# Attention, a spectral mix and an FFN on one core: one more chunk with seven block products, and a new order of the work

## Chip, cores and metric

The kernel runs on 1 core of one Trainium2 chip. The metric is the device time of one execution in microseconds, the median of several runs; a profile is one more execution, recorded by the hardware profiler.

## What is computed

Eight sequences of 576 positions, 8 heads of 64: windowed attention, whose output x (8 x 576 x 512) goes through a two-dimensional Fourier transform, a normalisation and an FFN of 512 to 2048 to 512. In float32 at the border:

```python
scores = np.where(mask, scale * np.matmul(q, k.transpose(0, 1, 3, 2)), -1e9)   # 0 <= row - col < 64
attn = np.exp(scores - max); attn = attn / (sum + 1e-09)
x = np.matmul(attn, v)                      # then heads side by side: 8 x 576 x 512
mixed = np.real(np.fft.fft(np.fft.fft(x, axis=1), axis=2))
u = x + mixed
un = (u - mu) / np.sqrt(var + 1e-06)
out = u + np.maximum(un @ w_ch1, 0.0) @ w_ch2
```

## The kernel before

The 4608 positions are 36 tiles of 128 (T0 to T35) and 18 chunks of two tiles (c0 to c17). `attn_tile(T)` loads k, q and v, turns k and q by the head dimension, makes scores, softmax and the product with v, and a first butterfly along the model dimension. `fft(b)` makes the two Fourier stages of one of the eight sequences and writes them to DRAM; `norm_tile(T)` gathers them back, adds, normalises and turns the result into the FFN's left operand. The first eleven tiles and chunk 0 work in float32; everything later in pairs of float16 (a high and a low part), and a product of two such pairs is three passes of matmuls (`PASSES`).

`ffn(c)` is the plain chunk: 16 first-layer steps `one` (12 matmuls of 256 columns each, L1419), ReLU into a high part on ScalarE (L1428) and a low part on VectorE (L1431), 16 second-layer steps `second` (6 matmuls of 512 columns, L1400), and one scaled addition for each of the two tiles (L1454).

`ffn7(c)` takes the chunks from `SEVEN` on. The hidden layer is cut in 8 pairs j of hidden blocks (`HALF`), the positions in two tiles, the outputs in two halves: 2 x 2 blocks, multiplied with seven block products instead of eight. The first layer is the same 192 matmuls (L1573). For each j ScalarE makes the ReLU (L1584), four sums of blocks follow on VectorE or GpSimd (`sums`, L1589), a cast to the high part on ScalarE or VectorE (`h_hi`), the low part on VectorE or GpSimd (`h_lo`, L1597), and then 7 products x 3 passes of 256 columns (L1548). The ending combines the blocks with one ScalarE step and seven VectorE additions. The sums of weight blocks, four of eight per j, are made once by `weight_sums(j)` (`sums` L1493, `more` L1500 to L1503, high parts by the copy helper L506, low parts L1511) and lie in `tw`, in buffers that attention used before (the staging of q, k, v, `flex`, `qbuf`, `kst`); the hidden tiles lie in the rings `kq`, `pr`, `pt`, `xe` and `yT`, which attention and the spectral stages use too.

```python
PROD = {1: (0, 0, 0), 6: (4, 0, 1), 7: (5, 1, 0), 5: (3, 3, 1), 2: (2, 2, 0), 3: (6, 2, 1), 4: (1, 3, 0)}
groups = (((0, 1, 2, 3), (1, 6, 7, 5, 4, 2, 3), 10),)      # product numbers of a middle j
for c in range(SEVEN, NCH):
    ffn7(c)
```

Nothing is ordered at run time. Every step is entered by `op(engine, duration, priority, function, reads, writes, ...)` and gets a running number; the table `ORDER` is the sequence in which all steps are issued, and `SECOND` names the steps that take the second of their two allowed engines. Every engine, and SyncE's queue with all its transfers, works its steps off in that order. `follow` walks the table and keeps the planner's own gap for each step; before the FFN begins, a planned gap of PE over 0.8 us is filled with matmuls into an unused bank (`warm`, L1759). Line numbers of the changed kernel are one higher behind the table.

Of the kernel before, what the change touches and what calls it, by code (L numbers as in the profile page):

```python
# [58 lines left out]
SEVEN = 12  # L59
# [339 lines left out]
def attn_fft_ffn_kernel(ctx: ExitStack, tc: tile.TileContext, q, k, v, w1, w2, gidx, dft_d, dft_s, mask, out):  # L399
# [1311 lines left out]
    for T in range(NTT):  # L1711
# [6 lines left out]
        if n in (4, 8):  # L1718
            base += FFT_AT + (FFT1 if T == 8 else 0)
            fft(2 * pb + n // 8, base)  # L1720
            for i, m in enumerate(range(0, 4) if n == 4 else range(4, 9)):
                args = NT * pb + m, base + NORM_AT + i + (EARLY if T == 4 and i > 1 else 0)
                if args[0] // 2 >= SEVEN + 4:
                    behind.setdefault(args[0] // 2, []).append(args)
# [66 lines left out]
```

## Time and profile before

| | us |
|---|---|
| median of 3 runs (944.35 to 948.38) | 944.51 |
| the profiled execution | 945.16 |
| its span, first to last instruction | 943.4 |
| TensorE matmul (PE) busy | 924.2 |
| VectorE (DVE) busy | 705.3 |
| GpSimd (POOL) busy | 441.5 |
| ScalarE (ACT) busy | 435.1 |

The busy times overlap each other. PE is TensorE's matmuls, PEld its loads of the stationary operand, SP the queue that issues nearly all transfers. A line such as `L1400 PE MATMUL po<-ws,hh` names the source line, the engine, and the tile written from the tiles read. The granted clock is given as a share of the full one; the DMA share is the mean busy share of the core's 16 DMA engines.

### The profile page before, as it was taken

To read this page: it belongs to the slowest core of one execution; us is meant where nothing else is said; L and a number is where in the kernel's file an instruction comes from. 1 tells how busy PE (TensorE), PEld (TensorE's weight loads), DVE (VectorE), ACT (ScalarE), POOL (GpSimd) and SP (SyncE) were. 2 spreads that over 40 slices of the span, in tenths; PEclk is the share of its full clock that TensorE was granted. 3 is DMA by queue.
4 is the path that set the end of the run, shared out by engine and by line. 5 is a ranking of instruction groups with operands and counts; after the bars stand their busy time and mean duration, and the time that the engine had idled before them with its cause. 6 is when DMAs were issued, how large, how long until landed. Compare 5 with 4: busy or idle time off the path is not lost.

```text
span 943.4 us, 24809 instructions
## 1 busy us (share of the span) xinstructions
PE 924.2 (98%) x9717; PEld 703.2 (75%) x9717; DVE 705.3 (75%) x1982; ACT 435.1 (46%) x979; POOL 441.5 (47%) x823
## 2 busy tenths in 40 slices
PE   7799999999999999999999999999999999999998
PEld 6677777666766676666766676667779998888887
DVE  5898998887767866677658757888898965675664
ACT  6875777834555424445443543444334442422111
POOL 2653464744744555465746544655601454124012
PEclk9999999999999999999999999999999999999999
DMA  9997447999689969879979788785402032210100
GB/s 231 239 263 202 133 144 147 167 173 169 136 193 163 198 122 167 185 152 207 197 168 190 150 162 169 163 147 108 137 12 57 24 96 65 68 35 13 57 24 23
DMA packets 300230, 128.69 MB, mean 136 GB/s; under 512 B 277768, under 2 KB 278152, under 8 KB 300112
## 3 DMA queue, kind: packets, MB, share of 16 engines
q1 hardware_dynamic: 297248, 118.06, 59.6%
q0 software_dynamic: 2720, 8.92, 3.3%
q8 instruction: 76, 1.25, 0.6%
q14 instruction: 42, 0.34, 0.1%
q10 hardware_dynamic: 144, 0.13, 0.0%
HBM read 60.76 MB, written 19.94 MB: 86 GB/s over the span
## 4 chain that ended last, share of the span: by engine, by line
PE 83%; DMA 5%; DVE 4%; POOL 3%; SPq 2%; issue 2%; ACT 1%; POOLq 0%; DVEq 0%; ACTq 0%
PE ph L1419 22%; PE po L1400 22%; PE ph L1573 13%; PE po L1548 11%; PE pz L1061 3%; PE pg L1023 3%; PE pa L739 3%; PE psc L662 2%; DMA kn<-in_k 1%; POOL flex L516 1%; DMA ve<-va 1%; DMA qn<-in_q 1%; DMA pt<-flex 1%; SPq L1277 1%; PE py L850 1%
## 5 line engine op out<-in xcount | busy, mean ns | idle before, releaser
L1400 PE MATMUL po<-ws,hh 128*128 128x512 f16 (+1 forms) x1116 | 284.5, 391 | 0.5 <-issue 0.2
L1419 PE MATMUL ph<-room,ws 128*128 128x256 f16 x2112 | 256.1, 273 | 1.8 <-DVE hh L1431 1.8
L1419 PEld LDWEIGHTS <-ws 128*128 128x128 f16 x2112 | 205.3, 98 | 54.1 <-issue 2.8
L1400 PEld LDWEIGHTS <-hh 128*128 128x128 f16 x1056 | 101.1, 98 | 90.0 <-DVE hh L1431 0.7
L1573 PE MATMUL ph<-room,ws 128*128 128x256 f16 x1152 | 136.2, 273 | 0.0
L1573 PEld LDWEIGHTS <-ws 128*128 128x128 f16 x1152 | 112.6, 98 | 13.6
L1428 ACT ACTIVATE hh<-ph 128x512 f16<-128x512 f32 x88 | 52.3, 594 | 120.8 <-PE ph L1419 99.8
L685 ACT ACTIVATE pr<-pr,nm 128x128 f32<-128x128 f32 x288 | 91.2, 393 | 31.5 <-DVE nm L677 31.4
L1431 DVE SCALAR_TENSOR_TENSOR hh<-ph,hh 128x512 f16<-128x512 f32 x88 | 60.4, 686 | 36.6 <-ACT hh L1428 36.5
L1135 POOL DMA_INDIRECT mt<-md,gix x34 | 42.0, 1235 | 96.7 <-DVE mv L1163 81.5
L677 DVE CUSTOM_DVE_ANT_0 pr<-psc,mskb 128x128 f32<-128x128 f32 x288 | 65.0, 287 | 25.9 <-PE psc L662 19.7
L1584 ACT ACTIVATE hx<-ph 128x512 f32<-128x512 f32 x47 | 27.8, 595 | 113.3 <-PE ph L1573 103.7
L1589 DVE TENSOR_TENSOR hx<-hx 128x128 f32<-128x128 f32 x164 | 45.1, 318 | 37.8 <-ACT hx L1584 36.2
L1548 PEld LDWEIGHTS <-hh 128*128 128x128 f16 x658 | 64.4, 98 | 7.6
L1597 POOL TENSOR_TENSOR hl<-hx,hh 128x256 f16<-128x256 f32 (+1 forms) x40 | 28.0, 730 | 77.3 <-DVE hh L510 53.7
L516 POOL TENSOR_TENSOR up<-un,up 128x128 f16<-128x128 f32 x84 | 40.9, 516 | 46.3 <-ACT up L506 38.8
L516 POOL TENSOR_TENSOR flex<-pr,flex 128x128 f16<-128x128 f32 x92 | 42.5, 494 | 36.2 <-ACT flex L506 18.2
L1548 PE MATMUL po<-ws,hh 128*128 128x256 f16 x282 | 51.2, 273 | 0.0
L1597 DVE TENSOR_TENSOR hl<-hx,hh 128x896 f16<-128x896 f32 x37 | 40.4, 1097 | 7.8 <-ACT hh L506 6.5
L752 POOL TENSOR_TENSOR rc<-rc,mone 128x4 f32<-128x4 f32 x29 | 32.5, 1129 | 26.6 <-DVE rc L747 16.8
L739 PE MATMUL pa<-ve,pt 128*64 128x65 f16 (+1 forms) x776 | 37.0, 203 | 2.5 <-ACT ve L506 1.8
L1548 PE MATMUL po<-ws,hl 128*128 128x256 f16 x141 | 38.4, 273 | 0.0
(244 smaller groups left out, 1718.6 us busy)
## 6 DMA issues: line engine op xcount, KB each, us to landing
room<-in_moe_w_ch SPq DMA_DIRECT2D x20, 512.0 KB
flex<-in_moe_w_ch SPq DMA_DIRECT2D x12, 512.0 KB
ve<-va SPq DMA_DIRECT2D x47, 130.0 KB
flex<-in_v SPq DMA_DIRECT2D x22, 256.0 KB
xs<-xu SPq DMA_DIRECT2D x22, 256.0 KB
xv<-xs SPq DMA_DIRECT2D x22, 256.0 KB
out<-xv SPq DMA_DIRECT2D x21, 256.0 KB
md<-mp SPq DMA_DIRECT2D x24, 192.0 KB
```

Of the source, the lines that this page charges most:

```text
L516: eng.tensor_tensor(out=out[:, k : k + w], in0=in0[:, k : k + w], in1=in1[:, k : k + w], op=al)
L677: nc.vector.tensor_tensor_reduce(out=t["pr", g][:, hp], in0=t["ps", g][:, hp], in1=mskb[:, m : m + P], scale=-0.125, scalar=3.0e38, op0=AL ...
L685: nc.scalar.activation(pr, pr, AF.Exp, bias=t["nm", g][:, hp : hp + 1], scale=-1.0)
L739: nc.tensor.matmul(pa[sl, hp], pt[:, sl], v_, start=(x == 0), stop=(x == len(mm) - 1))
L1400: nc.tensor.matmul(t["po"][i], l_, r_, start=(f == 0 and x == 0), stop=(f == NKF - 1 and x == len(mm) - 1))
L1419: nc.tensor.matmul(ph, l_, r_, start=(x == 0), stop=(x == len(mm) - 1))
L1428: nc.scalar.activation(t["hh", j][:, 0], ph, AF.Relu)
L1431: nc.vector.scalar_tensor_tensor(out=hh[:, 1], in0=ph, scalar=0.0, in1=hh[:, 0], op0=ALU.max, op1=ALU.subtract)
L1548: nc.tensor.matmul(t["po", bk][:, x], t["h", j][a][:, slot], right(n, j, b_), start=(j == 0 and k == 0 and n in opens), stop=(j == seven - ...
L1573: nc.tensor.matmul(ph, l_, r_, start=(x == 0), stop=(x == len(mm) - 1))
L1589: eng.tensor_tensor(out=x[:, o], in0=x[:, p0], in1=x[:, p1], op=al)
L1597: eng.tensor_tensor(out=lo[:, a:b_], in0=x[:, a + 1 : b_ + 1], in1=hi[:, a:b_], op=ALU.subtract)
```

## The change

`SEVEN` goes from 12 to 11, so chunk 11 is made by `ffn7` instead of `ffn`. With it the steps are numbered anew (3195 instead of 3178), the tables `ORDER` and `SECOND` are replaced as a whole, and no other line of the program differs. The first rows of the old and the new table:

```diff
@@ -56,151 +56,152 @@
 PASSES = ((0, 0), (0, 1), (1, 0))
 ONE = ((0, 0),)
-SEVEN = 12
+SEVEN = 11
 AWAY = 14
 
 ORDER = [int(i) for i in """
...
-1 115 0 9 7 116 3 15 118 119 120 145 121 124 144 129 16 149 125 130 173 126 131 147 150 117 127 148 17 132 21 18 176 153
...
+116 7 115 0 120 118 3 119 121 15 124 125 129 144 147 145 149 150 16 126 127 117 130 131 132 9 122 148 153 137 154 174
...
```

What the tables say, step by step: 69 steps of chunk 11 come and 52 go; 378 of the steps that both have change their engine, most between VectorE, ScalarE and GpSimd in attention, the spectral stages and the normalisation. Among PE's steps (771 before, 766 after) the first 140, up to the scores of T11, are the same work in nearly the same order. Behind them attention stands earlier: the scores of T24 have 348 PE steps ahead of them instead of 353, those of T30 444 instead of 460, those of T35 513 instead of 541. The first step of `weight_sums` stands beside chunk 9's FFN instead of chunk 10's.

## Rows read from the trace of the kernel before

**Rows 1.** The page: span and TensorE's busy time

```profile
span 943.4 us, 24809 instructions
...
PE 924.2 (98%) x9717; PEld 703.2 (75%) x9717; DVE 705.3 (75%) x1982; ACT 435.1 (46%) x979; POOL 441.5 (47%) x823
```

**Rows 2.** Busy time by stretch: opening, rest (stretch, length, engines with instruction counts, clock, DMA share, GB/s)

```profile
0.00:88.00 88.00, 77.05 (x949) 59.65 (x949) 69.61 (x267) 62.51 (x158) 45.19 (x83) 1.00 0.95 239
88.00:943.40 855.40, 847.14 (x8769) 643.52 (x8768) 635.68 (x1716) 372.64 (x822) 396.32 (x740) 1.00 0.60 126
```

**Rows 3.** PE's waits behind 88 us (us in total, times, longest)

```profile
PE ph L1419 <- DVE hh L1431: 1.8, 3, 1.3
PE psc L662 <- issue: 1.3, 3, 0.6
PE pa L739 <- DMA ve<-va: 0.5, 1, 0.5
...
```

**Rows 4.** The chain that ended last, its last piece (start, us, what)

```profile
939.45 0.75 DVE xv L1663
```

**Rows 5.** The same chain, one second-layer piece of each kind

```profile
621.96 2.59 PE po L1400 x12
...
712.22 2.29 PE po L1548 x21
```

**Rows 6.** Instruction groups by line (shapes, count, busy us, mean ns, idle before)

```profile
L1431 DVE SCALAR_TENSOR_TENSOR hh<-ph,hh 128x512 f16<-128x512 f32 x88 | 60.4, 686 | 36.6 <-ACT hh L1428 36.5
L1589 DVE TENSOR_TENSOR hx<-hx 128x128 f32<-128x128 f32 x164 | 45.1, 318 | 37.8 <-ACT hx L1584 36.2
L1597 DVE TENSOR_TENSOR hl<-hx,hh 128x896 f16<-128x896 f32 x37 | 40.4, 1097 | 7.8 <-ACT hh L506 6.5
L506 ACT CAST hh<-hx 128x896 f16<-128x896 f32 x24 | 22.5, 938 | 22.1 <-DVE hx L1589 21.3 <-POOL hx L1589 0.9
L1648 DVE SCALAR_TENSOR_TENSOR s<-po,osc,s 128x256 f32<-128x256 f32 x12 | 5.8, 481 | 1.2 <-ACT s L506 0.7
```

**Rows 7.** The tile of the weight sums (duration ns: min, median, max; first and last start)

```profile
L1493 DVE TENSOR_TENSOR td<-td,ws x16: 691/692/799, 614.2 to 723.5; 128x512 f32<-128x512 f32 x16
...
L1503 DVE TENSOR_TENSOR td<-td,ws x8: 424/424/536, 617.0 to 727.7; 128x256 f32<-128x256 f32 x8
L1511 DVE TENSOR_TENSOR flex<-td,flex x6: 677/684/691, 673.9 to 711.0; 128x512 f16<-128x512 f32 x6
```

**Rows 8.** Stretches around weight sums and chunk 12

```profile
620.00:740.00 120.00, 120.00 (x1126) 92.00 (x1125) 106.26 (x245) 45.69 (x92) 43.67 (x80) 1.00 0.36 82
...
720.00:740.00 20.00, 20.00 (x214) 18.13 (x213) 19.38 (x45) 8.26 (x13) 4.67 (x5) 1.00 0.14 33
```

**Rows 9.** The block sums by engine (duration ns: min, median, max)

```profile
L1589 DVE TENSOR_TENSOR hx<-hx x164: 280/287/760, 661.5 to 928.8; 128x128 f32<-128x128 f32 x164
L1589 POOL TENSOR_TENSOR hx<-hx x24: 449/456/1184, 765.6 to 923.3; 128x128 f32<-128x128 f32 x24
```

**Rows 10.** Stretches of attention: scores of T11 to T35, and two of 40 us

```profile
157.20:625.10 467.90, 463.73 (x5445) 326.70 (x5448) 342.12 (x1050) 224.45 (x538) 263.67 (x518) 1.00 0.87 169
160.00:200.00 40.00, 38.93 (x382) 25.40 (x380) 32.98 (x90) 28.59 (x57) 27.61 (x39) 1.00 0.96 163
...
440.00:480.00 40.00, 40.00 (x547) 29.90 (x545) 25.30 (x81) 20.16 (x53) 26.39 (x57) 1.00 0.99 191
```

**Rows 11.** The opening: a stretch, the weight conversions, the filler matmuls

```profile
40.00:50.00 10.00, 7.72 (x128) 5.80 (x126) 8.92 (x32) 7.68 (x19) 5.22 (x13) 1.00 1.06 282
...
L1289 DVE TENSOR_SCALAR ws<-room 128x1024 int32<-128x1024 int32 x10 | 7.1, 712 | 2.2 <-DMA room<-in_moe_w_ch 2.2
L1294 DVE SCALAR_TENSOR_TENSOR ws<-room,ws 128x1024 int32<-128x1024 int32 x10 | 12.4, 1238 | 0.3
L1301 DVE SCALAR_TENSOR_TENSOR ws<-room,ws 128x1024 uint16<-128x1024 uint32 x10 | 13.7, 1370 | 0.1
L1759 PE MATMUL warm<-ident 128*128 128x256 f16 x45 | 8.8, 325 | 1.5 <-POOL ident masks.py:199 1.5
```

277 rows, old and new, of tables (ORDER, SECOND) are left out of this document.

## The prediction

> **What bounds the kernel now.** I read the page's busy shares first, then stretches of the span, then what TensorE waited for, then the chain that ended last. The page says that TensorE (PE) is busy for 924.2 of 943.4 us [rows 1]. The stretches say where the other 19.2 us are: 10.95 before 88 us, in the opening, and 8.25 in the 855 us behind it, all at the full granted clock [rows 2]. What PE waited for behind the opening sums to about 4 us in waits of at most 1.3 us, most for the low half of the hidden layer (DVE hh) and for issue [rows 3]; the rest is the end, where the last VectorE step starts at 939.45 and the last transfer follows [rows 4]. So the kernel is its matmuls in sequence. An edit pays what it takes from PE, plus or minus what it does to 11 us of idle opening and 4 us of small waits; all other engines matter only where they begin to hold PE.
>
> The profiled execution took 945.16 us, of which 943.4 are the span; the median of the runs is 944.51, so 0.65 below it. I make the sum against 945.16 and take the 0.65 off at the end.
>
> **Part 1: chunk 11 takes seven products.** Its first layer keeps 192 matmuls of 256 columns. Its second layer had 16 steps of 6 matmuls of 512 columns; 12 such took 2.59 us, 0.216 each [rows 5], so 96 x 0.216 = 20.7. It becomes 8 x 7 products x 3 passes = 168 matmuls of 256 columns; 21 took 2.29, 0.109 each [rows 5]: 168 x 0.109 = 18.3. **PE: -2.4 us**, on the path, since PE has no wait there.
>
> The price is on the other engines. For each of 8 hidden blocks one VectorE low part of 0.69 goes; a sum step of 4 x 0.318 = 1.27 and a low part of 1.10 come, and ScalarE gets a cast of 0.94 [rows 6]: VectorE 8 x (2.37 - 0.69) = +13.4, ScalarE +7.5. The ending has seven output additions for two: three of 0.48, and four of 512 columns for two such, 0.69 each by the step that reads as much PSUM, some +3 [rows 6]. In the new table all eight of chunk 11's sum steps and low parts stand on VectorE. Cover: between the first step of the weight sums and the last low part that reads them, the old table has 145 VectorE steps beside 124.0 us of PE steps, the new one 135 steps beside 114.4. PE shrinks by 9.6 (eight FFN steps of 1.3 fewer, two attention products of 0.43 more); VectorE by only 5.1, at the mean durations of its rows. The weight sums themselves are the same (8 x (3 x 0.70 + 4 x 0.43 + 2 x 0.68)) [rows 7], only placed one chunk sooner. In the trace VectorE was busy 106.26 of 120 us from 620 to 740 while PE lost nothing, and 19.38 of 20 at the thickest [rows 8]. So 13.7 us of idle VectorE shrink by 9.6 - 5.1 = 4.5 to 9.2. I take this at nothing, because the row of 19.38 of 20 shows PE fed at a denser spot; if that cover is gone it costs up to 4.5.
>
> A trace row and a rule meet here. VectorE's sum instruction has a median of 287 ns, a mean of 318 and a longest of 760, which is the median plus 473, about one GpSimd sum (median 456) [rows 6, 9]. So a collision costs one GpSimd instruction, but on the mean only 31 ns: 32 instructions x 31 = 1 us, which is inside what I left idle. The Trainium skill (SBUF — State Buffer, "Who interferes with whom") says that a VectorE instruction with two SBUF inputs and a GpSimd instruction that reads SBUF exclude each other for a whole instruction. By that rule at its worst, all 32 sums waiting, it would be 32 x 456 = 14.6 us; the trace bears out the mechanism but not that frequency.
>
> **Part 2: attention comes sooner.** Nothing is added. Both tables have 140 PE steps ahead of tile 11's scores. Ahead of tile 35's the old one has 541, the new one 513: 26 FFN steps of 1.3 us and two attention products fewer, 34.8 us. It must be so, as the hidden tiles and the combined weights of the seven-product chunks reuse attention's buffers. So the attention tiles, the spectral stages and their transfers, 467.9 us long in the trace [rows 10], get about 433 us; the waits of SyncE's one queue, which carries every load, transpose and store in order, get as much shorter. The transfers' mean share of 0.87 becomes 0.87 x 467.9 / 433 = 0.94. Bounds: one stretch had 0.99 and PE lost nothing in it, one had 0.96 and PE lost 1.07 in 40 us [rows 10]. So from -4.2 (all idle in this stretch gone, 467.9 - 463.73) to 433 / 40 x 1.07 - 4.2 = +7.4. I take **0**: the row at 0.99 is the nearest to 0.94 with little slack, the present waits are redrawn by a new order rather than removed, and there is no row that says to which side.
>
> **Part 3: the opening.** The order of PE steps is nearly the same: 79 steps ahead of the first FFN step in both tables. Ahead of it stand 50 transfers instead of 54; gone are one weight load of 512 KB, two loads of 256 KB and a small one. At the 239 GB/s of the opening [rows 2] that is 2.2 + 2 x 1.1 = 4.4 us of a transfer system that is over-full there (1.06) [rows 11]. Against it VectorE gets the three conversions of one more weight pair, 0.71 + 1.24 + 1.37 = 3.3 [rows 11], and four copies out of PSUM from ScalarE, 2.7 at the 0.69 of a VectorE step that reads as much PSUM [rows 6], less about 1 for small steps: +5, and it is busy 8.92 of 10 there [rows 11]. Bounds -4.4 and +5; I take **0**, as neither is nearer. The 45 filler matmuls (8.8 us) [rows 11] lie in PE's waits; their number follows the order's planned gaps and I can't read it from the diff. Cost nothing, as they fill waits.
>
> **Part 4: the end.** The last PE steps have the same order. One addition into the last tile moves from VectorE (0.7) to GpSimd; it has the last 4.6 us of products (30 of 0.109 and 6 of 0.216) to end in. Taken at nothing.
>
> **Sum:** 945.16 - 2.4 = 942.8 for a profiled execution, and less 0.65: **942.1 us**.
>
> **Rivals.**
> 1. The new order also removes idle PE: transfers release the opening. The first column of the FFN comes 4.4 us sooner: 942.1 - 4.4 = **937.7**. For: four transfers fewer ahead of the first FFN step, and 10.95 us of idle PE to take from. Against: most of PE's waits there are not ended by a transfer, and VectorE gets more work.
> 2. VectorE holds PE in chunk 11. If VectorE needs the 13.7 us of idle it has now, for hand-overs with ScalarE and PE, the stretch grows by 4.5: 942.1 + 4.5 = **946.6**, slower than before. The place is the stretch of weight sums and chunk 11; it decides for slower once more than 2.4 of the 4.5 come through. For: the hand-over chain has ScalarE and VectorE in turn, four steps a block. Against: 19.38 of 20 without a wait of PE. By the skill's rule above at its worst it would be further out; the mean of the row speaks against that.
> 3. VectorE holds the opening: +5, **947.1**. For: 8.92 of 10 busy. Against: the extra conversions can slide behind the first FFN step.
> 4. Transfers are late all through attention: +7.4, **949.5**. For: 0.94 on the mean leaves little slack. Against: 0.99 in a stretch where PE lost nothing.
>
> **How the numbers follow.** Chances: forecast 0.47 (its own range 940 to 944.5), rival 1 0.26, rival 2 0.13, rival 3 0.07, rival 4 0.07. Leaving out the far end of rival 1 and rival 4, the range is 936.5 to 948. A measurement here can tell about 0.5% from no change, that is 939.8 and 949.2. Faster: rival 1 and a little of the forecast, 0.28. Slower: rival 4 and combinations of 2 and 3, 0.11. Same: 0.61.
>
> **What would show it.** Right: PE's busy time near 921.8 with the same count of fillers, seven-product matmuls in seven chunks, waits of PE behind the opening still about 4 us and none over 2. Rival 1: PE idle before 88 us well under 10.95, and the first FFN matmul sooner. Rival 2: PE waits ended by VectorE or ScalarE on the products of chunk 11, with VectorE at 0.95 or more around them. Rival 3: more idle PE before 88 us, ended by VectorE. Rival 4: PE waits in scores and attention products ended by transfers, with the share above 0.95. The prediction is wrong in its mechanism if the time changes by more than 3 us with PE's busy time down by 2.4.

## The result: slower, 953.97 us

| | before | after |
|---|---|---|
| median of the runs, us | 944.43 | 953.97 (951.95 to 956.1) |
| ratio, with 95% interval | | 1.0108 (1.0085 to 1.0131) |
| profiled execution / its span, us | 945.16 / 943.4 | 951.95 / 950.2 |

The change costs 9.5 us where 2.4 us of gain were forecast; the time lies above the range. The profiled execution is the fastest of the changed kernel's six; it is 6.8 us above the profiled one of the kernel before, so the traces account for 6.8 of the 9.5 us. The chips used differ a little (medians of the kernel before from 943.6 to 946.5), so experiments are compared by their ratio to runs of the kernel before on the same chip.

The page, the two stretches of [rows 2] and PE's waits behind 88 us, in the kernel after:

```profile
span 950.2 us, 25037 instructions
PE 923.9 (97%) x9786; PEld 711.6 (75%) x9786; DVE 719.4 (76%) x2009; ACT 441.4 (46%) x992; POOL 457.0 (48%) x850
```

```profile
0.00:88.00 88.00, 75.38 (x947) 59.52 (x948) 69.31 (x247) 60.93 (x157) 41.18 (x79) 1.00 0.93 235
88.00:950.20 862.20, 848.47 (x8841) 652.12 (x8839) 650.08 (x1763) 380.47 (x835) 415.84 (x771) 1.00 0.60 125
```

```profile
PE psc L663 <- DMA kst<-flex: 4.2, 2, 2.9
PE psc L663 <- DMA ve<-va: 2.3, 1, 2.3
PE py L851 <- POOL y L517: 1.8, 1, 1.8
PE ph L1574 <- DVE hh L1432: 0.3, 1, 0.3
...
```

Against [rows 1 to 3]: PE is idle 12.6 us before 88 us (10.95 before) and 13.7 behind it (8.25 before), 7.1 us more in all, and its busy time is only 0.35 lower, though 2.4 us of products and some 0.9 us of filler matmuls (42 for 45) are gone. The waits behind the opening are few and long: 1.8 at 94 us for a butterfly on GpSimd, 1.3 at 196 us and 2.9 at 226 us for the transposed k of a score, 2.3 at 360 us. After the two longest the granted clock falls (the 5 us behind 225, and behind 360), so that part of each stretch ran at 1.2 GHz instead of 2.4. By an estimate from these rows (3.40 x 0.34 + 5.00 x 0.30) this cost 2.7 us, which is most of the busy time that should be gone:

```profile
220.00:225.00 5.00, 3.57 (x67) 2.47 (x64) 4.26 (x12) 2.04 (x6) 3.46 (x6) 1.00 1.39 206
225.00:230.00 5.00, 3.40 (x58) 2.68 (x59) 2.19 (x5) 1.59 (x4) 0.22 (x1) 0.66 0.71 160
360.00:365.00 5.00, 5.00 (x68) 3.41 (x68) 3.90 (x21) 0.16 (x1) 4.92 (x12) 0.70 1.00 194
```

The chain of waits into the two scores shows the same sequence twice (start, us, what): GpSimd subtracts the last low half; the transposing transfer of k stands in SyncE's queue behind other issues (L594 at 188.60 is that of q, L716 that of a softmax tile) and starts 1.8 and 1.3 us later; it lands 6.0 us behind the start of its issue.

```profile
186.33 1.28 POOL flex L517 x3
...
187.72 0.43 POOL flex L517
...
188.60 1.29 SPq L594
...
189.94 6.00 DMA kst<-flex
...
195.98 0.86 PE psc L663 x48
...
217.49 1.80 POOL flex L517 x4
219.29 0.55 SPq L716
...
220.53 0.03 SPq L594
...
220.59 5.96 DMA kst<-flex
...
226.59 1.49 PE psc L663 x33
```

These are tiles 13 and 15. Read in the two tables, with PE steps at their durations, the last subtraction of a low half of k or q stands 6.1 us of PE work ahead of the score in both, the shortest distance of all tiles in the new order; in the old one the shortest is 6.3 by the same durations (tile 11; the expectations below have 6.7), and tiles 13 and 15 have 11.3 and 10.0. What has to fit in is subtraction, the wait in the queue, issue and landing: 9.6 us from 186.33 to 195.98, 9.1 from 217.49 to 226.59. The sums by which orders are written in this program put 1.5 + 2.6 us on that transfer (`TURN` and its `lat`). The wait of 2.3 us at 360 us is another matter: it is put down to a copy of v, which a score doesn't read, and in `cut_216us` below the same score's wait is ended by VectorE.

So the theory: the new order leaves its k and q less time than the transfers take, and its opening is a little longer. The rivals: the chunk of seven products itself (VectorE); attention that is sooner as such, with transfers pressed together (the fourth rival of the prediction); the opening alone.

### The profile page after: what moved, and what is told of

Its sections match the earlier page's. It is cut to its first block, busy times and chain, and to the rows that moved or that the text cites. A ratio compares the mean times of both kernels' runs of the same rounds, so it can differ in the third digit from the quotient of the medians.

```text
span 950.2 us, 25037 instructions
## 1 busy us (share of the span) xinstructions
PE 923.9 (97%) x9786; PEld 711.6 (75%) x9786; DVE 719.4 (76%) x2009; ACT 441.4 (46%) x992; POOL 457.0 (48%) x850
## 4 chain that ended last, share of the span: by engine, by line
PE 75%; DMA 5%; DVE 3%; POOL 3%; issue 2%; SPq 1%; ACT 1%; POOLq 0%; ACTq 0%; DVEq 0%
PE po L1401 19%; PE ph L1420 18%; PE ph L1574 15%; PE po L1549 13%; PE pz L1062 2%; PE pg L1024 2%; PE psc L663 2%; PE pa L740 2%; DMA pt<-flex 2%; POOL flex L517 1%; DMA kst<-flex 1%; DMA py<-yp 1%; DMA room<-up 0%; POOL mt L1136 0%; PE py L851 0%
## 5 line engine op out<-in xcount | busy, mean ns | idle before, releaser
L1401 PE MATMUL po<-ws,hh 128*128 128x512 f16 (+1 forms) x1020 | 262.3, 393 | 0.4 <-ACT hh L1429 0.3
L1429 ACT ACTIVATE hh<-ph 128x512 f16<-128x512 f32 x80 | 47.4, 593 | 92.7 <-PE ph L1420 63.8
L1590 DVE TENSOR_TENSOR hx<-hx 128x128 f32<-128x128 f32 x196 | 53.4, 314 | 44.0 <-ACT hx L1585 41.9
L1432 DVE SCALAR_TENSOR_TENSOR hh<-ph,hh 128x512 f16<-128x512 f32 x80 | 54.8, 686 | 31.8 <-ACT hh L1429 31.3
L1598 DVE TENSOR_TENSOR hl<-hx,hh 128x896 f16<-128x896 f32 x41 | 45.6, 1115 | 28.4 <-ACT hh L507 22.2
L1598 POOL TENSOR_TENSOR hl<-hx,hh 128x256 f16<-128x256 f32 (+1 forms) x56 | 37.8, 703 | 51.1 <-DVE hh L511 27.0
L1549 PE MATMUL po<-ws,hh 128*128 128x256 f16 x330 | 60.0, 273 | 0.0
L517 POOL TENSOR_TENSOR flex<-pr,flex 128x128 f16<-128x128 f32 x72 | 34.5, 508 | 31.3 <-DVE flex L511 23.3
L1549 PE MATMUL po<-ws,hl 128*128 128x256 f16 x165 | 45.0, 273 | 0.0
L663 PE MATMUL psc<-kst,qbd 64*64 64x128 f16 (+1 forms) x1552 | 35.2, 237 | 8.1 <-DMA kst<-flex 4.2
```

Of the source, the lines that this page charges most:

```text
L517: eng.tensor_tensor(out=out[:, k : k + w], in0=in0[:, k : k + w], in1=in1[:, k : k + w], op=al)
L663: nc.tensor.matmul(t["ps", g][64 * jj : 64 * jj + 64, hp], qT[rows, 4 * a + hp, 64 * jj : 64 * jj + 64], keys(4 * b_ + hp, jj, rows), star ...
L1401: nc.tensor.matmul(t["po"][i], l_, r_, start=(f == 0 and x == 0), stop=(f == NKF - 1 and x == len(mm) - 1))
L1429: nc.scalar.activation(t["hh", j][:, 0], ph, AF.Relu)
L1432: nc.vector.scalar_tensor_tensor(out=hh[:, 1], in0=ph, scalar=0.0, in1=hh[:, 0], op0=ALU.max, op1=ALU.subtract)
L1549: nc.tensor.matmul(t["po", bk][:, x], t["h", j][a][:, slot], right(n, j, b_), start=(j == 0 and k == 0 and n in opens), stop=(j == seven - ...
```

## Experiments

**The old order up to a cut.** Four kernels with seven chunks take the steps of the old order, with its engines, up to a cut, and the rest in the new order. (Here and below such an edit is shown by the rule that made it; in the kernel it is a new `ORDER` and `SECOND`. These tables differ in length, so L663 of the changed kernel is L668 in some of the others.)

```diff
-order = new
+head = [s for s in old[:cut] if s in new]        # cut = 580, 850, 1520, 2420
+order = head + [s for s in new if s not in head]
```

> Chunk 11 keeps its seven products; the first 580 steps of the order (up to about 148 us of the trace) are those of the kernel before, with its choices of engine, the rest are the changed kernel's. Four kernels of this series differ only in how far the old order reaches (580, 850, 1520, 2420 steps of 3195). Theory (late transfers at four places: PE held at 94, 196, 226 and 360 us of the changed kernel's trace, 1.8 + 1.3 + 2.9 + 2.3 us, each with some time at half clock, and an opening 1.7 us longer): this one takes back the opening and the 94 us place, 3.5 us, so about 949 to 950 against the changed kernel's 954. Rival, the opening is the whole cause: 944 less 2.4 for the seven products, about 942, in all four kernels. Rival, the chunk of seven products is itself what costs: 954 in all four.

> As the first, but the old order reaches 850 steps, to about 216 us of the trace, past the second place (196 us) and most of what leads to the third (226 us). Theory of the four places: 3.5 + 1.3 + 2.9 us and about 2 us of half clock come back, so about 944 to 946. Rival, opening alone: as the first kernel. Rival, the chunk of seven products: 954.

> As the first, but the old order reaches 1520 steps, to about 380 us, past all four places; the last twelve attention tiles still come as in the changed kernel's order. Theory of the four places: all of the loss comes back and the seven products' 2.4 us stay, so 941 to 943, below the kernel before. Rival, it is the sooner attention as such (more transfers for each us, wherever it is): the tiles still to come are pressed together even more, so 946 to 950. Rival, the chunk of seven products: 954.

> As the first, but the old order reaches 2420 steps, to about 620 us, so all scores but those of the last tile come when they came before; only what lies behind, chunk 11's seven products among it, is the changed kernel's. Theory of the four places and of the sooner attention alike: the gain of the seven products alone, about 942 (944.4 less 2.4). Rival, the chunk of seven products is itself what costs (VectorE or the tail): 946 to 954.

| cut | median, us | ratio |
|---|---|---|
| 580 | 952.03 | 1.0089 (1.0054 to 1.0124) |
| 850 | 948.71 | 1.0056 (1.0040 to 1.0071) |
| 1520 | 957.64 | 1.0159 (1.0129 to 1.0188) |
| 2420 | 970.98 | 1.0297 (1.0266 to 1.0328) |

The first two go as the theory says in direction, short of its size: both lie above the ranges expected. The old order up to 216 us gives back some 5 us. The old opening alone gives back some 2, which isn't clear of the noise, as its interval overlaps the changed kernel's. The other two miss every expectation, and the waits say why. The seam itself costs: the one long wait of the third kernel stands 33 us behind its cut (about 380 us), and in the fourth PE lost 20 us between 560 and 720 us, around its cut at 620.

```profile
413.10 0.26 PE L745 MATMUL pa<-ve,pt 128*64 128x65 f16 x1 [14.10 <-DMA pt<-flex]
```

In the opening cut PE was 5.1 us ahead of the kernel after by 160 us (79.13 + 71.64 us busy, against 75.38 + 70.24) and lost most of that at tile 13 and later. What is gained ahead of a place that is late is waited for there.

In `cut_216us` the score that the changed kernel held for 2.3 us at 360 us waits 2.9 us, for VectorE, and the granted clock stays full behind it:

```profile
355.03 0.98 PE L668 MATMUL psc<-kst,qbd 64*64 64x128 f16 x48 [2.89 <-DVE mp L1086]
```

```profile
355.00:360.00 5.00, 4.97 (x76) 3.66 (x77) 3.96 (x22) 0.08 (x1) 4.92 (x12) 1.00 0.97 179
```

**Softer mixtures and one local move.** In `late_two_scores` the two scores stand four PE steps later:

```diff
 av T11 g1
-score T13
 second c1 f13
 ffn c2 j0 f0
 second c1 f14
 ffn c2 j0 f1
+score T13
```

> The changed kernel with one edit of its order: the scores of tiles 13 and 15 (the two at which PE was held for a transpose of k, 1.3 us at 196 us and 2.9 us at 226 us) come four PE steps, about 5 us, later, behind FFN work that is ready; what needs them moves along. In the new order these two tiles have the shortest distance of all from the subtraction that makes their low half to their score, 6.1 us of PE work; the tiles of the old order have 6.7 to 35. Theory (too short a lead, not a lack of transfer): both holds go, and about a microsecond of half clock with them, and do not come back elsewhere: 947 to 950 against the changed kernel's 954. Rival (the 16 DMA engines are full from 190 to 450 us, so what PE gains at one place it waits at the next): 952 to 955.

It took 959.68 us, 1.0147 (1.0121 to 1.0172): slower still. Both waits for k are gone, and others stand in their place (PE's waits from 160 to 260 us):

```profile
PE ph L1425 <- DVE hh L1437: 3.7, 2, 2.7
PE pa L745 <- DMA ve<-va: 2.4, 1, 2.4
PE ph L1425 <- DMA room<-up: 1.0, 1, 1.0
```

The mask and the softmax of these tiles moved back with their scores, and on VectorE the FFN's low halves stand behind them. The expectation failed: a score can't be moved alone, since what follows it is queued on four engines.

The other three place each step by a weighted mean of its ranks in both orders (`place = w * new.index(s) + (1 - w) * old.index(s)`).

> Chunk 11 keeps its seven products. Each step is placed by a weighted mean of its places in the two orders: the old order alone up to step 1500 (about 375 us), the new order alone from step 1900 (about 475 us), and a slow change between. It differs from the cut at 1520 steps, which was held 14.1 us at 413 us, in having no hard seam. Theory (short leads at 94, 196, 226 and 360 us): as fast as the old kernel up to 400 us and the seven products' 2.4 us below it after, so 941 to 944. Rival, sooner attention as such costs wherever it is: 946 to 950. Rival, the chunk of seven products costs by itself: 952 to 956.

> Chunk 11 keeps its seven products. Each step is placed half way between its places in the two orders up to step 2300 (about 575 us), then the order changes slowly to the new one. The shortest lead of tiles 13 and 15 is 8.7 us of PE work in it. Theory (short leads): no hold at 196 and 226 us, half of what the opening cost, 942 to 946. Rival, sooner attention as such (DMA share): half of the loss, about 949. Rival, seven products: 952 to 956.

> The kernel before, chunk 11 with its eight plain products, but with the new order up to step 1000 (about 250 us), the old order from step 1400 (about 345 us) and a slow change between. Theory (short leads and the new opening): the holds at 94, 196 and 226 us and the 1.7 us of the opening come into a kernel that has no seventh chunk of seven products, 6 us of holds and 1 to 3 us of half clock: 950 to 954. Rival, the chunk of seven products is what costs: 944. Rival, the sooner attention from 250 to 620 us is what costs: 944 to 947.

They took 969.91, 1038.19 and 966.55 us (1.0241, 1.0947 and 1.0217). All three miss every expectation and are worse than either order they are made of, by waits in the mixed stretch (in `half_way`, 18.8 us for the FFN's low halves alone). The first two decide nothing on the cause. The third does up to 280 us, where its order is hardly mixed yet (the stretch from 88 to 280 us, first in the kernel before, then after, then this one):

```profile
88.00:280.00 192.00, 190.82 (x1857) 135.45 (x1857) 159.78 (x418) 120.59 (x263) 102.76 (x177) 1.00 0.73 157
...
88.00:280.00 192.00, 185.52 (x1803) 130.95 (x1802) 156.28 (x419) 119.70 (x261) 99.84 (x186) 0.99 0.76 154
...
88.00:280.00 192.00, 186.27 (x1816) 131.29 (x1811) 156.91 (x421) 119.01 (x261) 97.26 (x183) 0.99 0.74 155
```

PE loses 4.6 of the 5.3 us of this stretch in a kernel whose chunk 11 is plain. The early loss is the order's, not the seven products'.

**Transfers of k and q that land sooner.** This leaves both orders as they are and changes what they wait for:

```diff
 def turn_(two=two, dst=dst):
-    nc.sync.dma_start_transpose(dst, two.rearrange("p z c -> p (z c)"))
+    nc.sync.dma_start(dst.rearrange("p h s -> p (h s)"), two.rearrange("p z c -> p (z c)"))
```

> The kernel before; the transposing transfers of k and q in tiles 11 to 35 (flex to kst and to qbd) are replaced by plain copies of the same bytes, so scores are taken of halves that aren't transposed; everything else and the order stay. The two transposes at which the changed kernel was held landed 6.0 us behind their issue, plain copies in SBUF (ve from va) 2.8 us. Both theories: the old order leaves these transfers 6.7 us of PE work or more, and PE hardly waits for them, so little changes: 940 to 944.

> The changed kernel with the same replacement: plain copies of k and q in place of the transposing ones in tiles 11 to 35. Theory: the new order stands or falls with how soon these transfers land (it was written for a landing some 4 us behind the issue; 6 us and more is what they take), directly at 196 and 226 us and, through engines that work in their queue's order, behind them. So the loss goes nearly whole: 938 to 944, no slower than the kernel before with the same replacement. Rival (the opening and the press of all other transfers and in-order engines cost the same as before): 1.8 + 1.7 us of the opening and the later holds stay, 948 to 952, and 7 us or more above the other kernel of this pair.

The kernel before stays as it is, 944.04 us, 0.9999 (0.9982 to 1.0015). The kernel after comes down to 948.86, 1.0038 (1.0018 to 1.0058): 0.70% of the 1.08% are gone, which is 6.6 us by the ratios and 5.1 by the medians. The theory's 938 to 944 failed: the time is in the rival's range, with 4.8 us above the other kernel of the pair instead of the rival's 7. So more than half of the loss goes with these transfers, and not all of it. From 160 to 240 us PE is busy 78.12 us instead of 75.28:

```profile
160.00:240.00 80.00, 75.28 (x858) 51.29 (x847) 63.72 (x191) 48.64 (x107) 42.82 (x75) 0.98 0.87 163
...
160.00:240.00 80.00, 78.12 (x898) 53.43 (x897) 66.43 (x197) 51.46 (x111) 44.90 (x79) 1.00 0.76 165
```

The copies change three things at once: they land sooner, each holds SyncE's queue for 0.53 to 0.57 us instead of 1.30 to 1.36 (medians for k and q in this kernel and in the kernel after), and the DMA share falls. The last is tested below; the first two were not taken apart.

**The old opening on top of it**, the cut at 580 steps and the plain copies together:

> The changed kernel with both edits: the old order up to step 580 (about 148 us) and plain copies of k and q in place of the transposing transfers in tiles 11 to 35. Theory (two causes that add up, the opening with 3.4 us and the late k and q with 5): 942 to 945, level with the old kernel with the same copies (944.0) or below it by up to the 2.4 us of the seven products. Rival (what the old opening gains is waited for at later places whatever the transfers of k and q take, as in the run with the old opening alone): 947 to 950.

944.93 us, 1.0012 (0.9994 to 1.0030): another 0.26%, 2.5 us by the ratios and 3.9 by the medians. The theory's range holds: the two edits together take back 0.96 of the 1.08%. That the old opening gives back more here than alone, because no late k holds PE behind it, is not shown; the intervals are as wide as the difference. That the opening costs something is shown by the traces: the score of tile 11, with 140 PE steps ahead of it in both orders, starts at 156.0 to 159.2 us in the nine profiled kernels with the old opening, and at 159.7 to 164.2 us in the five with the new one (157.2 in the kernel before, 159.7 in the kernel after).

Its page and waits behind 88 us, and the waits of the old kernel with the same copies below them:

```profile
PE 921.6 (98%) x9789; PEld 709.5 (75%) x9789; DVE 716.5 (76%) x2013; ACT 441.8 (47%) x989; POOL 469.2 (50%) x862
```

```profile
PE po L1406 <- DVE hh L1437: 1.7, 2, 1.2
PE psc L668 <- ACT g L512: 1.1, 1, 1.1
PE ph L1425 <- DVE hh L1437: 1.1, 3, 0.4
PE psc L668 <- DVE xu L764: 1.0, 1, 1.0
PE pa L745 <- DMA pt<-flex: 0.8, 2, 0.4
PE ph L1579 <- DVE hh L1437: 0.4, 1, 0.4
```

```profile
PE psc L662 <- issue: 0.9, 2, 0.5
PE ph L1419 <- DVE hh L1431: 0.5, 1, 0.5
```

Here the seven products can be seen at last: PE's work is 921.6 us, 2.6 below the 924.2 of [rows 1], at the same 45 fillers and the full clock. But PE waits 6.1 us behind 88 us where the old order has 1.4, for VectorE and ScalarE more than for transfers. In this kernel the gain of the products is given back there.

**Fewer bytes.** Is it the press of transfers that makes them late?

```diff
-nc.sync.dma_start(t[nm][o : o + m], ap)
+few = slice(0, 2 if T >= PRO + 4 and (i or nm == "vn") else H)
+nc.sync.dma_start(t[nm][o : o + m, few], ap[:, few])
```

> The changed kernel, order and transposes as they are; from tile 15 on the loads of v, and of k and q in odd tiles, bring 2 of the 8 heads instead of all (the rest of the buffer keeps what an earlier tile left), which is half of attention's load bytes. Theory (the sooner attention presses the transfers together, and that is what makes k and q land 6 us and more behind their issue): the DMA share from 200 to 600 us falls by some 0.1, the hold at 226 us shrinks, and 3 to 5 us of the 9.5 come back: 949 to 951. Rival (the landing takes as long without the press, only the distance that the order leaves counts): 952.5 to 955.

> The kernel before with the same cut of loads. Both theories: the old order leaves its transfers room, so hardly anything changes, 942.5 to 945; it stands beside the other kernel so that a general effect of fewer bytes is seen.

952.25 us, 1.0069 (1.0046 to 1.0092), and 943.72, 0.9983 (0.9965 to 1.0001). Between the two kernels 8.5 us stay of 9.5, though the DMA share from 200 to 600 us (first after, then this kernel) fell below the 0.87 that attention has in the kernel before [rows 10]:

```profile
200.00:600.00 400.00, 394.51 (x4772) 280.23 (x4771) 303.74 (x949) 189.28 (x471) 234.44 (x464) 0.99 0.92 177
...
200.00:600.00 400.00, 391.51 (x4683) 278.14 (x4682) 302.70 (x956) 188.21 (x468) 231.92 (x461) 1.00 0.84 159
```

The median falls just short of the rival's range, the ratio (951 us) at the theory's end; the pair says that the mean share explains about 1 us by the medians and 2 by the ratios, neither clear of the noise. The changed kernel with plain copies has nearly the same share in this stretch and is 3.4 us faster (1.0038 against 1.0069, intervals that overlap a little), so the share is hardly what it gains by:

```profile
200.00:600.00 400.00, 396.30 (x4802) 281.33 (x4800) 307.49 (x982) 191.98 (x475) 238.90 (x472) 1.00 0.83 180
```

In `light_after` the waits for k are gone and others have come (2.0 for a copy of v at 230 us, 1.4 for the FFN's low half at 210), as in `late_two_scores`.

**Orders with more room.** Both orders were rearranged step by step (mean shift about 16 places) so that by the kernel's own planning sums they end soonest when k and q land 1.75 us later than these sums had it, and in the last two also when the other transfers do (1.2 us for the other transposes, 0.6 for loads):

```diff
-order = new            # or old, or the cut at 850
+order = rearranged(order, landing of k = 1.5 + 2.6 + 1.75, of q = 1.5 + 2.2 + 1.75)
```

> The changed kernel, chunk 11 with its seven products, nothing left out; its order is rearranged step by step (mean shift 16 places, 317 other choices of engine) so that by the kernel's own planning sums, with k and q landing 1.75 us later than these sums had it, it ends soonest; the tiles that had 6.1 us from the low half to the score now have 8.7 us and more. Theory (late k and q, and an order that had no room for them, are the cause): the loss goes, 938 to 944. Rival (crowding of the DMA engines or the opening or the seven products themselves): 948 to 956.

> As the kernel before this one, chunk 11 with seven products and nothing left out, but the rearranging started from the mixed order (old order up to step 850, new order behind), so its opening is nearly the old one. Theory: 937 to 943, and not slower than the one that started from the new order. Rival (crowding or the seven products): 947 to 954.

> The kernel before, chunk 11 with eight plain products, its order rearranged in the same way with the same later landing. It tells what of a gain comes from the rearranging alone. Theory (the seven products are worth 2.4 us where the order has room): 939 to 945, and 1 to 3 us above the two rearranged kernels with seven chunks. Rival (the seven products give nothing, the gain is all of the rearranging): the same time as theirs within 0.5 us or below.

> Chunk 11 with seven products, nothing left out, the order of replan_mixed rearranged once more so that its planned end stays where it is when k and q land up to 2.5 us, the softmax's transposes 1.2 us and the loads 0.6 us later than planned; the shortest lead from a low half to its score is 8.4 us of PE work. Theory (seven products gain 2.4 us of PE work, and it shows where no transfer or in-order engine holds PE): 939 to 941.5, and 1.5 to 2.5 us below the order with six chunks. Rival (sooner attention has its own price on VectorE and ScalarE whatever the order): 941.5 to 944, level with the order with six chunks.

> The kernel before, chunk 11 with eight plain products, nothing left out, its order rearranged in the same way with the same room for the transfers. Theory: 941 to 943, above the one with seven chunks by 1.5 to 2.5 us. Rival: level with it within 0.5 us.

| | chunk 11 | median, us | ratio |
|---|---|---|---|
| replan_after | seven products | 950.80 | 1.0065 (1.0034 to 1.0096) |
| replan_mixed | seven products | 942.77 | 0.9986 (0.9971 to 1.0001) |
| room_seven | seven products | 949.20 | 1.0037 (1.0018 to 1.0057) |
| replan_before | plain | 942.13 | 0.9975 (0.9959 to 0.9991) |
| room_six | plain | 941.47 | 0.9957 (0.9942 to 0.9972) |

`replan_mixed`, in which nothing is left out, takes all of the loss back; the other two with seven products miss their expectation and stay at +0.4 to +0.7%. In both sets the kernel with a plain chunk 11 was expected to be slower by 1 to 3 us, and it is faster: by 0.6 and 8.7 us in the first, where the rival had said so, and by 7.7 us in the second. The fastest version of all has a plain chunk 11: `room_six`, 0.43% below the kernel before.

`replan_after` shows where the rest went. It keeps the sooner attention, and with longer distances (and other choices of engine) PE loses only 0.7 us from 200 to 600 us, at a higher DMA share than in the kernel after (5.5 us at 0.92):

```profile
200.00:600.00 400.00, 399.28 (x4830) 283.41 (x4828) 301.24 (x930) 195.94 (x488) 247.19 (x481) 1.00 0.94 182
```

What stays is its opening, which comes from the new order (12.2 us of idle PE before 88 us), and waits for VectorE in the stretch of the weight sums and chunk 11, 1.9 us in two between 600 and 640 us and 2.5 at 657 us. So the loss inside attention can go while attention comes as soon and its transfers are pressed as much.

The only waits of `room_six` behind 88 us (first two lines below) are short. `room_seven` has more; the longest is for VectorE, and one of 0.9 us shows a transposing transfer that landed 10.3 us behind the start of its issue, most of that in 10 us with a DMA share of 1.25 (the head of the same list, a piece of the chain of waits, and a stretch of `room_seven`):

```profile
PE py L854 <- POOL y L520: 1.1, 1, 1.1
PE pz L1065 <- DVE g L1034: 0.3, 1, 0.3
```

```profile
PE py L856 <- DVE y L522: 2.9, 1, 2.9
PE psc L668 <- DVE mp L1086: 1.0, 1, 1.0
PE pa L745 <- DMA pt<-flex: 0.9, 1, 0.9
PE psc L668 <- DMA qbd<-flex: 0.9, 1, 0.9
...
```

```profile
418.99 10.32 DMA qbd<-flex
```

```profile
420.00:430.00 10.00, 9.10 (x135) 6.58 (x135) 7.08 (x14) 2.94 (x9) 8.05 (x17) 1.00 1.25 136
```

So a 1.75 us longer landing doesn't cover the slowest transfers. That orders with seven products lose more because their transfers stand closer is not shown: `replan_mixed` has the highest share of them all (0.95 from 200 to 600 us) and loses nothing. That the 2.4 us of the products come out at the end in some order isn't shown: none of the kernels with seven chunks was faster than its counterpart with a plain chunk 11.

## Why the prediction was wrong, step by step

**Part 1, seven products: right in size, and its rival fell in this order.** The 2.4 us were measured as 2.6 of PE work (in `plain_opening`). The second rival, VectorE holding chunk 11, is contradicted for the changed kernel: from 620 to 740 us PE was busy all but 0.7 us, with VectorE at 102.68 of 120 against the 106.26 of [rows 8].

```profile
620.00:740.00 120.00, 119.32 (x1094) 98.46 (x1091) 102.68 (x231) 46.44 (x91) 46.51 (x83) 1.00 0.28 71
```

In `replan_after`, where PE loses hardly anything in attention, it comes true in part: the waits of 1.9 us before 640 us and of 2.5 at 657 us are of its kind and at its place.

The block sums collide with GpSimd no more than before, with a mean of 314 ns in place of 318 [rows 6] and a longest of 761:

```profile
L1590 DVE TENSOR_TENSOR hx<-hx 128x128 f32<-128x128 f32 x196 | 53.4, 314 | 44.0 <-ACT hx L1585 41.9
```

With the rule weighed there (the Trainium skill, SBUF — State Buffer, "Who interferes with whom") this again agrees in the size of one collision: 761 is the median of 286 and 475 more, and a GpSimd sum has a median of 453. The worst case worked out from it, every sum waiting, did not come.

**Part 2, attention sooner: this is the step that failed.** Its facts held. The scores of tiles 11 to 35 take 438.6 us (433 forecast), the DMA share is 0.91 (0.94 forecast):

```profile
159.70:598.30 438.60, 431.42 (x5167) 304.69 (x5166) 335.47 (x1032) 217.24 (x527) 256.99 (x504) 0.99 0.91 176
```

But the term was put at 0 between -4.2 and +7.4, by the row with a share of 0.99 in which PE lost nothing. In the profiled execution it cost some 5.7 us: PE is idle 7.2 us in this stretch instead of 4.2, and the lower clock takes an estimated 2.7. By the medians, 9.5 of loss and 2.6 of products less the opening's 2.5 to 3.9 leave 8 to 10 us, more than the upper bound; 5.1 to 6.6 of them go with the transposing transfers of k and q.

What counted wasn't the share but the order. The prediction counted how many steps stand ahead of each score and never how many stand between a score and what feeds it: 6.1 us in tiles 13 and 15, against some 9 that subtraction, queue and landing took there. The distance alone would not have named these two places. Tile 11 of the kernel before has hardly more, 6.3 us, and PE waits for no k there [rows 3]; and in four traces that show when every k and q landed, this took 3.5 to 4.4 us in the median, near the planner's sums, and 4.9 to 7.4 at the longest (`cut_216us`, `replan_before`, `replan_mixed`, `replan_after`). At the two places a short distance met a slow landing.

The Trainium skill (DMA: Bandwidth & Descriptors, "Latency and other measured facts") has 261 GB/s for a transposing transfer with a non-contiguous middle dimension; by that figure the 256 KB of one tile's k would take an estimated 1.0 us. That is a rate and no time to landing: here 6.0 and 10.3 us passed from issue to landing in the slow cases, and an order has to be fitted to these.

**Part 3, the opening: mis-sized.** Taken as 0 between -4.4 and +5; it cost 2.5 us by the ratios (3.9 by the medians), and in the two traces 1.7 us more idle PE before 88 us and the 1.8 at 94 us, where the butterfly of tile 7 had gone from VectorE to GpSimd. The third rival (VectorE holds the opening) was right in kind at a part of its price: before 88 us VectorE now ends waits of PE that sum to 4.8 us, where they were 1.9; the longest two are

```profile
PE py L851 <- DVE xu L759: 1.5, 1, 1.5
...
PE pa L740 <- DVE ve L511: 1.1, 1, 1.1
```

The four transfers fewer, on which the first rival rested, did not shorten the idle time.

**Part 4, the end: right**; PE is idle 4.1 us in the last 70.2 us of the span, 4.0 before.

**The rivals and the bounds.** The fourth rival, transfers late all through attention, 949.5 us at a chance of 0.07, was the nearest: the place and the releasers (waits of scores for k, above 2 us) are as it named them. Its cause, a high mean share, is worth 1 to 2 us at most. Two terms had bounds of both signs and were set to 0 as if independent, though both come from one new order; both went to the bad side. And the text gave no price to a lower clock, which in the profiled execution took an estimated 2.7 us.

**Open**: how the 2.6 us of PE work are given back when k, q and the opening are mended. Waits for VectorE and ScalarE are there, but no run took them away; moving single scores only moved them. Open too is how much of what the plain copies give back comes from sooner landing and how much from the shorter issues on SyncE's queue, and what the 2 us are by which the median of the changed kernel lies above its profiled execution.

## What to carry to other kernels

Where an order is written by hand or by a planner, measure for each kind of transfer the time from issue to landing in the busiest stretch, its slow cases too, and look for the readers with the shortest distance to it; the mean share of the DMA engines said little here. Before counting a gain on the bounding engine, ask what must come sooner to make room for it: here 2.4 us of products needed attention 35 us sooner, and that cost more than they gave. An order that was fitted closely doesn't mix with another: every mixture but the two with an early cut was slower than both parents.

## What the runs showed of the hardware

Transposing transfers of 256 KB within SBUF (k and q) landed 3.5 to 4.4 us behind their issue in the median of four runs; those at which PE was held took 6.0 us, landing at 196 and 226 us, and one took 10.3 us in a fuller stretch (DMA share 1.25). Each took SyncE's queue 1.30 to 1.36 us, a plain copy of the same bytes 0.53 to 0.57. After single waits of 2.9 and 2.3 us TensorE's granted clock was 0.66 and 0.70 in the 5 us rows behind them, so part of each ran at 1.2 GHz. The length of a wait doesn't decide it alone: behind the 2.9 us in `cut_216us` the clock stayed at 1.00, and behind one of 1.7 us at 224.6 us in `replan_mixed` it was 0.66:

```profile
225.00:230.00 5.00, 5.00 (x34) 3.00 (x27) 4.19 (x9) 2.35 (x4) 4.57 (x7) 0.66 0.81 160
```

`room_six` and `plain_opening`, with no single wait over 1.2 us behind 88 us, have the full clock in nearly all stretches.
